# Message passing on a graph: fixed PSUM banks, overlapping stages and paired adding scatters in a kernel that sorts edges by target while it multiplies them

## The chip, the core and the metric

The kernel runs on one core of a Trainium2 chip. The metric is device time in microseconds (us), the median of three runs. The engines are TensorE (PE in the profile, its weight loads PEld), VectorE (DVE), ScalarE (ACT), GpSimd (POOL) and SyncE (SP, which only issues transfers here). POOL issues the indirect transfers: gathers and scatters whose rows are named by a list of indices.

## The reference: one layer of a message-passing network

```python
N, deg, D, De = 12500, 64, 64, 16
E = N * deg                                   # 800,000 edges
def reference(x, e_attr, src, dst, w_msg, w_upd):
    m_in = jnp.concatenate([x[src], x[dst], e_attr], axis=-1)
    msg = _silu(m_in @ w_msg)                 # (E, 64)
    agg = _segment_sum(msg, dst, N)           # (N, 64)
    return _silu(jnp.concatenate([x, agg], axis=-1) @ w_upd)
```

Everything is float32; `src` and `dst` are random, so an edge may go from any node to any node.

## The kernel before

The product with `w_msg` is split. `A = x @ w_msg[0:64]` is computed once per node and kept in DRAM (`A_d`); an edge gathers its source's row of it. The part of the target node and of the edge's attributes is a product of its own, with weights `BW` that hold 98 target nodes (a *bucket*; there are 128 buckets) and the 16 attribute rows. For this the edges have to lie sorted by bucket, and the kernel sorts them itself, with matrix products, while it works on those that are sorted already.

**Sorting.** 782 steps take 8 tiles of 128 edges each. A step makes a one-hot matrix of the buckets (`onehot`, ACT L396/L397), counts with bf16 matmuls which edge is the how-manieth of its bucket (`count`, PE, tile `z`), takes the rank by a maximum (`ranks`, DVE L433), spreads each edge's record of 17 floats to the slot of its rank (`expand`, DVE L446, tile `X`), and multiplies with the one-hot matrix (`move`, PE L463, tile `pl`), so that each of the 128 buckets has its records in one row of PSUM. The products of 8 tiles (the first 140 *chunks*) or of 12 (the other 428) are summed there. ACT copies the row block out (`blk`, L468), DVE moves each bucket's pointer on (`place`, L481/L482), and POOL scatters the 128 rows behind the buckets' ends in the store `st` in DRAM (L486): 24 or 30 records a row. A bucket that gets more records than a row holds loses the chunk, which is then redone at the end.

**Messages.** From the store, *groups* of 24 to 64 sorted tiles are taken. A group is formed over several periods (`k` = 0, 1, 2, ...): DVE computes how many whole units of 1, 2 or 4 tiles each bucket holds; a matmul with a triangular matrix (L581) makes running sums; three small matmuls make the *work list* (L585 to L587: the tile, the column of `BW` and the column of the sum for each unit), which DVE copies into `row` and `rb` (L592, L593); SP reads addresses from it and loads the tiles (`rt`). A group is worked on in *batches* of 8 tiles (6 in the second stage). A batch passes through four periods: 8 gathers by POOL (L649) and the one-hot matrix `q` of the targets within the bucket (DVE L659); transposes on PE (`tq`, L668), copied out by ACT (`qt`, L671), and the product `pre` with BW (PE L677); the sum with the gathered rows and SiLU (DVE L681, ACT L682); the reduction over targets by PE (`ag`, L698), added into `ACC` in SBUF (DVE L710).

**Order.** The program is issued exactly as it is written, engine by engine. One `period` holds a sort step and a batch, each in its present phase of the pipeline, in this order: four gathers, the scatter, four gathers; one-hot matrices; the small vector work of a group that is forming (`fourth`); counts; transposes and their copy; reduction; ranks; message; `add`; `expand`; `move`; `product`; the rest of `move`; `place`; the list matmuls of a forming group (`middle`). A planner written in Python decides before the program is built in which period a group starts, from 16 random draws of how full the buckets are. The early stages are 48 tiles one by one, then groups of 24 tiles two by two until each bucket has given its share, then groups of 64 tiles four by four; a stage starts when the one before has been taken whole. After the last sort step the left-over tiles run in a tail without sorting.

**PSUM.** Six pools of one buffer each hold `z`, the constants' bank `cb`, `pl`, `tq`, `pre` and `ag`. The work list's tile `ps` comes from the pool of `ag`:

```python
g.ps = pag.tile([P, 512], F32, name="ps2", tag="ag")     # the list of a forming group
t.ag = pag.tile([P, 512], F32, name="ag")                # the sums of a batch
```

so a list is written only when the sums before it have been added, and the next sums only when the list has been copied out. Four buffers of gathered rows are used in turn: the first gather into one waits for the last matmul of the `ag` that read it (`t.older`). Each matmul of `ag` is on record in `t.gathers`.

Of the kernel before, what the change touches and what calls it, by code (L numbers as in the profile page):

```python
# [14 lines left out]
P = 128  # L15
# [14 lines left out]
XR = 2 + W  # L30
# [6 lines left out]
FIRST = [(1, 48, BT, (1, 0, 1, 0)), (2, 24, 6, (3, 3, 2, 2))]  # L37
# [7 lines left out]
SUMMED = "the sum that this reads waits for the gathers into its buffer, the older ones there were read ahead of them"  # L45
LISTED = "the work list holds buckets and tiles of the store"


def mpnn_kernel(tc, x, e_attr, src, dst, w_msg, w_upd, out):
# [7 lines left out]
    CAPT = (K8 * S8 + (NCH - K8) * S) // P + 2  # L57
# [3 lines left out]
    NREC = TOP * P  # L61
# [11 lines left out]
    with es:  # L73
# [4 lines left out]
        pz = pool("pz", 1, space=PSUM)  # L78
        pc = pool("pc", 1, space=PSUM)
        pp = pool("pp", 1, space=PSUM)  # L80
        pt = pool("pt", 1, space=PSUM)
        ppre = pool("ppre", 1, space=PSUM)
        pag = pool("pag", 1, space=PSUM)

        A_d = dr.tile([NB * BK, D], F32, name="A_d")
        XU_d = dr.tile([BK, NBK * D], F32, name="XU_d")
        st = dr.tile([NREC, R], F32, name="st")
        st_t = st.rearrange("(t e) c -> t (e c)", e=P)

# [32 lines left out]
        cb = pc.tile([P, 512], F32, name="cb")  # L122
        ioB = cb[:, 0:BK]
        ioS = cb[:, BK:BK + S]
        hit = cb[:, P:P + M * S].rearrange("p (k s) -> p k s", s=S)
# [3 lines left out]
        nc.vector.tensor_scalar(out=ioS, in0=iof[:, 0:S], scalar1=RK, scalar2=None, op0=OP.add)  # L129

# [7 lines left out]
        ub = {u: cp.tile([NBK, 1], F32, name=f"ub{u}") for u in (1, 2, QU)}  # L138
        nc.vector.tensor_scalar(out=ub[1], in0=ipf, scalar1=float(CAPT), scalar2=None, op0=OP.mult)
        ptr0 = cp.tile([NBK, 1], I32, name="ptr0")  # L140
        nc.vector.tensor_scalar(out=ptr0, in0=ub[1], scalar1=float(P), scalar2=None, op0=OP.mult)
# [3 lines left out]
        capm = cp.tile([NBK, 2 + len(FIRST)], F32, name="capm")  # L145
# [8 lines left out]
        stages = []  # L154
        for i, (u, gt, bt, give) in enumerate(FIRST):
# [7 lines left out]
            stages.append(dict(u=u, gt=gt, bt=bt, cap=cap, caps=caps, total=u * sum(caps)))  # L163
        stages.append(dict(u=QU, gt=GT, bt=BT, cap=None, caps=None, total=None))
# [5 lines left out]
        class Nodes:  # L170
# [20 lines left out]
            def turn(t):  # L191

                xt_p = pt.tile([P, BT * P], F32, name="xt_p", tag="t")
# [9 lines left out]
            def parts(t, i):  # L203
                ps = (ppre, pag)[i % 2].tile([P, 512], F32, name="abp", tag=("pre", "ag")[i % 2])
# [132 lines left out]
        ACCf = ACC.rearrange("p b k -> p (b k)")  # L337
        for t in X:
            nc.gpsimd.memset(t[:, :, 0:1], 1.0)
        nc.gpsimd.memset(sent, 0.0)  # L340
# [6 lines left out]
        def later():  # L347
# [5 lines left out]
            if len(zeros) == 15:  # L353
                for k in range(P // SR):
# [7 lines left out]
        bp = pool("bp", 2)  # L362
        sm = pool("sm", 4)
        rcp = pool("rcp", 2)
# [6 lines left out]
        state = dict(x=0, rt=0, u=1, ptr=ptr0, done=done0, stage=0, taken=0, straight=True)  # L371

        blocks = []
        gathers = []
        live = []

        prior = dict(step=None, pl=None)

        class Step:


            def __init__(c, hi, rec, index, n=M):

                c.hi, c.rec, c.n = hi, rec, n
# [4 lines left out]

                c.last = {k: K8 + (index * M + k) // c.size for k in range(n) if c.pos[k] == c.size - 1}  # L390
# [27 lines left out]
            def count(c):  # L418

                hb = c.hf.bitcast(BF16).rearrange("p m (b two) -> p m b two", two=2)[:, :, :, 1]  # L420
                c.z = pz.tile([P, M, NBK], F32, name="z")
# [293 lines left out]
        def period(step=None, batch=None, ptr_new=None):  # L715
# [49 lines left out]
            if p:  # L765
                p.move(1)
# [420 lines left out]
```

## Time and profile before

| | |
|---|---|
| three runs | 10704.04, 10711.36, 10720.38 us; median 10711.36 |
| span of the profiled execution | 10886.0 us, at a mean granted TensorE clock of 0.885 |
| busy, share of the span | PE 82%, DVE 66%, POOL 60%, PEld 57%, ACT 47% |
| moved by DMA | 501.15 MB, 46 GB/s |
| gathers, scatters | 6322 and 568 |
| batches (copies `qt`), groups (pairs of list copies) | 818, 115 |

The profiled execution took 1.6% longer than the median of the three runs. In rows of groups, the number after x counts instructions; a float32 matmul is two records on PE, so 12644 records of `ag` are 6322 matmuls. Behind the bar stand the busy time in us and the mean of one in ns, then the time that the engine was idle just before, with what ended it. "remote" is a semaphore event that the profile doesn't put down to one instruction, "issue" is idle time in which the engine waited for nothing that the profile shows. Rows by stretch of time show the length, the busy time of each engine with its number of instructions, the granted clock, the share of the DMA engines' time and GB/s.

### The profile page before, as it was taken

How to read it: one execution, taken by the hardware profiler on the slowest of the kernel's cores; microseconds unless marked ns; L12 is line 12 of the kernel's file. 1: busy time of each engine (PE TensorE's matmuls, PEld its weight loads, DVE VectorE, ACT ScalarE, POOL GpSimd, SP SyncE). 2: the span in 40 equal slices, each digit the busy share in tenths (PEclk: the TensorE clock that was granted, in tenths of full speed). 3: DMA queues.
4: the chain of work that ended last, by engine and by line, in shares of the span. 5: the costliest groups of instructions: out<-in, count | busy, mean ns of one | idle time of the engine just before them, and what ended most of it. 6: DMA issues, size and time to landing. Idle time of an engine off the chain costs nothing. (4 is left out here: it accounts for less than half of the span.)

```text
span 10886.0 us, 155616 instructions
## 1 busy us (share of the span) xinstructions
PE 8949.9 (82%) x49053; PEld 6219.2 (57%) x49816; DVE 7231.4 (66%) x15936; ACT 5082.6 (47%) x12594; POOL 6571.4 (60%) x6908
## 2 busy tenths in 40 slices
PE   8788888888888888888888888888888888888556
PEld 5566655555555555555555555555555555555555
DVE  7777776666666666766666666666666666766232
ACT  6455554444444444444444444444444444544211
POOL 2565666666666666666666666666666666666555
PEclk9999998999989988999998999999899998988555
DMA  3111111111111111111111111111111111111212
GB/s 97 44 49 48 49 49 46 43 47 42 47 42 46 45 44 45 44 43 44 46 43 46 44 44 43 46 47 43 45 42 46 43 47 44 44 45 41 46 36 44
DMA packets 662903, 501.15 MB, mean 46 GB/s; under 512 B 492983, under 2 KB 529911, under 8 KB 662071
## 3 DMA queue, kind: packets, MB, share of 16 engines
q0 software_dynamic: 238976, 349.72, 12.3%
q1 hardware_dynamic: 422775, 141.27, 5.9%
q8 instruction: 400, 6.55, 0.3%
q14 instruction: 432, 3.54, 0.1%
q10 hardware_dynamic: 320, 0.07, 0.0%
HBM read 330.05 MB, written 152.30 MB: 44 GB/s over the span
## 5 line engine op out<-in xcount | busy, mean ns | idle before, releaser
L649 POOL DMA_INDIRECT g<-A_d,sidx x6322 | 5997.6, 949 | 3658.7 <-issue 1620.7
L463 PE MATMUL pl<-X,hf 128*128 128x291 f32 (+5 forms) x12512 | 4745.0, 524 | 476.4 <-issue 428.3
L463 PEld LDWEIGHTS pl<-X,hf 128*128 128x128 f32 x12512 | 2538.7, 211 | 2159.4 <-issue 1737.4
L446 DVE TENSOR_TENSOR X<-cb,rec 128x442 f32<-128x442 f32 (+5 forms) x3128 | 2646.6, 908 | 26.7
L396 ACT ACTIVATE hf<-iof,shi 128x128 f32<-128x128 f32 x6256 | 1908.8, 389 | 1360.4 <-PE pl L463 449.0
L671 ACT ACTIVATE qt<-tq 114x1024 f32<-114x1024 f32 (+1 forms) x818 | 811.7, 992 | 2951.3 <-remote 2298.5
L433 DVE TENSOR_REDUCE rank<-z 128x8 f32<-128x1024 f32 x782 | 954.5, 1221 | 1270.3 <-remote 874.9
L677 PEld LDWEIGHTS pre<-w,qt 114*128 114x128 f32 x10496 | 1392.5, 209 | 687.8 <-ACT qt L671 467.1
L677 PE MATMUL pre<-w,qt 114*128 114x64 f32 x10496 | 1395.2, 291 | 345.6 <-ACT qt L671 317.6
L710 DVE TENSOR_TENSOR ACC<-ag,ACC 64x98 f32 x1938 | 496.7, 256 | 1553.3 <-remote 1131.7
L698 PE MATMUL ag<-q,g 128*64 128x98 f32 x12644 | 882.3, 276 | 490.4 <-remote 236.2
L698 PEld LDWEIGHTS ag<-q,g 128*64 128x64 f32 x12644 | 681.6, 151 | 668.8 <-issue 381.7
L668 PE MATMUL tq<-ident,q 128*114 128x128 f32 x6322 | 929.9, 294 | 103.3 <-issue 91.5
L668 PEld LDWEIGHTS tq<-ident,q 128*114 128x114 f32 x6322 | 812.6, 147 | 238.7 <-issue 122.6
L397 ACT ACTIVATE hf<-hf,ones 128x1024 f32<-128x1024 f32 x782 | 898.8, 1149 | 25.4
L486 POOL DMA_INDIRECT st<-blk,ptrs x567 | 567.2, 1000 | 561.4 <-ACT blk L468 272.2
L659 DVE TENSOR_TENSOR q<-cb,lo 128x784 f32<-128x784 f32 (+1 forms) x818 | 768.7, 940 | 96.1 <-PE ag L698 46.3
L468 ACT ACTIVATE blk<-pl 128x512 f32<-128x512 f32 (+1 forms) x568 | 324.9, 572 | 818.2 <-PE pl L463 500.9
L426 PE MATMUL z<-G,onesb 128*128 128x384 bf16 x1564 | 529.8, 339 | 78.9 <-issue 25.2
L682 ACT ACTIVATE g<-g 128x512 f32<-128x512 f32 (+1 forms) x818 | 498.4, 609 | 192.5 <-DVE g L681 111.8
L681 DVE TENSOR_TENSOR g<-pre,g 128x512 f32<-128x512 f32 (+1 forms) x818 | 541.3, 662 | 51.4 <-issue 37.2
L677 PE MATMUL pre<-BW,qt 114*128 (+1 forms) x2148 | 326.3, 314 | 99.0 <-ACT qt L671 64.8
(138 smaller groups left out, 5243.9 us busy)
## 6 DMA issues: line engine op xcount, KB each, us to landing
g<-A_d,sidx POOLq DMA_INDIRECT x6322
ea<-in_e_attr SPq DMA_DIRECT2D x260, 192.0 KB
rt<-st SPq DMA_DIRECT2D x1312, 34.0 KB
st<-blk,ptrs POOLq DMA_INDIRECT x567
rt<-st SPq DMA_DIRECT2D x434, 8.5 KB
nodes<-in_x SPq DMA_DIRECT2D x62, 98.0 KB
ACC<-rt SPq DMA_DIRECT2D x11, 544.0 KB
rt<-st SPq DMA_DIRECT2D x320, 17.0 KB
```

Of the source, the lines that this page charges most:

```text
L396: nc.scalar.activation(c.hf[:, k, :], iof, AF.Square, bias=c.hi[:, k:k + 1])
L397: nc.scalar.activation(c.hf, c.hf, AF.Relu, bias=ones, scale=-1.0)
L433: nc.vector.tensor_reduce(out=c.rank, in_=c.z, axis=AX.X, op=OP.max)
L446: nc.vector.tensor_tensor(out=c.x[:, k:k + 2, 2:2 + n * R].rearrange("p k (s c) -> p k s c", c=R), in0=hit[:, k:k + 2, 0:n, None].to_broad ...
L463: nc.tensor.matmul(pl[:, 0:w], c.hf[:, k, :], c.x[:, k, 0:w], start=(n == (c.size - 1 if whole else 0)), stop=ends, skip_group_check=True)
L486: i = nc.gpsimd.indirect_dma_start(out=st, out_offset=bass.IndirectOffsetOnAxis(ap=c.ptr, axis=0), in_=c.blk[:, 2:], in_offset=None)
L649: j = nc.gpsimd.indirect_dma_start(out=t.g[:, i, :], out_offset=None, in_=A_d, in_offset=bass.IndirectOffsetOnAxis(ap=t.grp.sidx[:, k:k + ...
L659: nc.vector.tensor_tensor(out=t.q[:, 0:n, 0:BK], in0=ioB[:, None, :].to_broadcast([P, n, BK]), in1=t.grp.lo[:, i0:i0 + n, None].to_broadca ...
L668: nc.tensor.transpose(t.tq[0:KQ, j * P:(j + 1) * P], t.q[:, j, :], ident)
L671: nc.scalar.activation(t.qt[:, 0:w], t.tq[0:KQ, 0:w], AF.Copy)
L677: nc.tensor.matmul(t.pre[:, i * D:(i + 1) * D], t.qt[:, i * P:(i + 1) * P], w, start=True, stop=True)
L698: o = nc.tensor.matmul(t.ag[t.half(v), v // 2 * BK:(v // 2 + 1) * BK], t.g[:, i, :], t.q[:, i, 0:BK], start=(k == 0), stop=(k == u - 1))
```

## The change

There are three parts.

1. **PSUM tiles are held for good.** `z`, `tq`, `pl`, `pre`, `ag` and `cb` are allocated once. The work list gets columns 400 to 512 of the `ag` bank to itself when it has at most 112 entries; a longer one still takes the whole bank (64 units at one tile each have 192). With it, the matmuls of `ag` are no longer on record one by one: one more matmul per batch, eight columns by one, stands behind them and is what gathers and additions wait for.
2. **Stages overlap.** The single tiles come first and are 192, in groups of 12, 12 and 24 tiles with batches of 6. Each stage keeps its own account of what it has taken, and in each period the first stage that has enough for a group starts one. The groups of four-tile units are 32, 32, 32 and then 64 tiles.
3. **Chunks past step 140 go to the store in pairs.** The first of two chunks is laid flush right in a row of 30 records, the second flush left in the 30 beside it, and one scatter writes rows of 60 records so that both lie end to end behind the bucket's end. What lies around them are zeros, and the scatter adds to what is in DRAM instead of overwriting it. The rows have to hold zeros beforehand: SP copies a block of zeros (`Z_d`, 128 rows of 4080 bytes) to each part of the store, four parts ahead. A pair in which a bucket lost records is scattered aside.

```diff
+XR = 2 + W + 2
+ROW = 2 * S
+LEAD = 4
-FIRST = [(1, 48, BT, (1, 0, 1, 0)), (2, 24, 6, (3, 3, 2, 2))]
+FIRST = [(1, (12, 12, 24), 6, (2, 1, 2, 1)), (2, (24,), 6, (3, 3, 2, 2))]
+LATER = (32, 32, 32, GT)
...
-        pag = pool("pag", 1, space=PSUM)
+        ps = pool("ps", 1, space=PSUM)
+        zb = ps.tile([P, M, NBK], F32, name="z")
+        tb = ps.tile([P, BT * P], F32, name="tq")
+        plb = ps.tile([P, 512], F32, name="pl")
+        preb = ps.tile([P, 512], F32, name="pre")
+        agb = ps.tile([P, 512], F32, name="ag")
...
+        def fill():
+            a = (P - S + len(filled) * ROW) * R
+            z = nc.sync.dma_start(st_b[:, a:a + ROW * R], Z_d)
...
+            def keep(c, pl, right):
+                if c.single or c.side == 0:
+                    prior["cnt"] = sm.tile([NBK, 8], F32, name="cnt")
...
+                if c.main:
+                    nc.scalar.activation(c.cnt[:, c.side, :], pl[:, f:f + 2], AF.Copy)
+                c.blk = BLK[:, c.side, 0:n]
+                nc.scalar.activation(c.blk, pl[:, a:a + n], AF.Copy)
...
             def scatter(c):
-                i = nc.gpsimd.indirect_dma_start(out=st, out_offset=bass.IndirectOffsetOnAxis(ap=c.ptr, axis=0), in_=c.blk[:, 2:], in_offset=None)
+                if c.single:
+                    i = nc.gpsimd.indirect_dma_start(out=st, out_offset=at, in_=c.blk, in_offset=None)
+                else:
+                    i = nc.gpsimd.indirect_dma_start(out=st, out_offset=at, in_=BLK.rearrange("p a w -> p (a w)"), in_offset=None, compute_op=OP.add)
...
+        def listing(n):
+            return agb[:, 4 * BK + 8:512] if n <= 504 - 4 * BK else agb
...
-                    g.ps = pag.tile([P, 512], F32, name="ps2", tag="ag")
+                    g.ps = listing(3 * gu)
...
             def reduce(t):
-                t.ag = pag.tile([P, 512], F32, name="ag")
+                t.ag = agb
...
-                            o = nc.tensor.matmul(t.ag[t.half(v), v // 2 * BK:(v // 2 + 1) * BK], t.g[:, i, :], t.q[:, i, 0:BK], start=(k == 0), stop=(k == u - 1))
-                            t.gathers.append(o.ins)
+                            nc.tensor.matmul(t.ag[t.half(v), v // 2 * BK:(v // 2 + 1) * BK], t.g[:, i, :], t.q[:, i, 0:BK], start=(k == 0), stop=(k == u - 1))
+
+                o = nc.tensor.matmul(t.ag[0:t.n, 4 * BK:4 * BK + 1], t.g[:, 0:t.n, 0], ones, start=True, stop=True)
+                t.gathers.append(o.ins)
...
-            if size() and may_start() and draws.holds(state["u"], size() // state["u"]):
...
+            if may_start():
+                for g in stages:
+                    n = size(g)
+                    if n and draws.holds(g, n):
+                        draws.take(g, n)
+                        start_group(g, state["ptr"], n)
+                        break
```

How the instructions stand, at three places. First, PE behind the list of a forming group (L585 to L587 write the list of 16 units, `z` counts, `tq` transposes, `ag` is the reduction). Before:

```order
L585 MATMUL ps_33559<-mat,wl 1x16 [waits DVE_49]
L586 MATMUL ps_33559<-mat,b_102 1x16
L587 MATMUL ps_33559<-mat,b_104 1x16
L428 LDWEIGHTS onesb
L428 MATMUL z<-G,onesb 128x512 [waits DVE_49]
L668 MATMUL tq<-ident,q 114x128 x8
L698 MATMUL ag<-q,g_223 64x98 [waits DMASW6_49,DVE_49,PE_49]
L698 MATMUL ag<-q,g_223 64x98 [waits DMASW3_49]
```

The same place now, where the list is L677 to L679, the reduction L790 and the added matmul L792:

```order
L677 MATMUL ag<-mat,wl 1x16 [waits DVE_49]
L678 MATMUL ag<-mat,b_93 1x16
L679 MATMUL ag<-mat,b_95 1x16
L475 LDWEIGHTS onesb
L475 MATMUL z<-G,onesb 128x512 [waits DVE_49]
L760 MATMUL tq<-ident,q 114x128 x8
L790 MATMUL ag<-q,g_233 64x98 [waits DMASW1_49,DVE_49]
L790 MATMUL ag<-q,g_233 64x98 [waits DMASW0_49]
L792 MATMUL ag<-ones,g_233 8x1
L516 MATMUL pl<-X_193,hf 128x359 x2
```

The wait of `ag` for PE's own list matmuls is gone, and what its wait for DVE now stands for is no longer the copies of the list, only the messages and the additions of the batch before. The matmul L792 is new in every batch.

Second, POOL in the stretch with both kinds of work (`st` is the store, `g` gathered rows). Before, and in most periods:

```order
L486 DMA st<-blk,ptrs 2938112x17 [waits DMASW3_49,DMASW4_49,DVE_49,Activation_49]
L649 DMA g_220<-A_d,sidx 128x64
L649 DMA g_220<-A_d,sidx 128x64 [waits DMASW5_49]
L649 DMA g_221<-A_d,sidx 128x64 [waits DMASW6_49,PE_49]
L649 DMA g_221<-A_d,sidx 128x64 [waits DMASW7_49]
L649 DMA g_221<-A_d,sidx 128x64 [waits DMASW0_49]
```

Now, with an adding scatter in every third period, which also waits for a fill of zeros (DMAHW):

```order
L570 DMA st<-BLK,cnt 2994944x17 [waits DMASW1_49,DMAHW0_49,DVE_49,Activation_49]
L741 DMA g_234<-A_d,sidx 128x64 [waits DMASW2_49]
L741 DMA g_234<-A_d,sidx 128x64 [waits DMASW3_49]
L741 DMA g_234<-A_d,sidx 128x64 [waits DMASW4_49]
L741 DMA g_234<-A_d,sidx 128x64 [waits DMASW5_49]
L741 DMA g_235<-A_d,sidx 128x64 [waits DMASW6_49,PE_49]
```

The semaphores DMASW0 to DMASW7 are taken in turn, so that each gather waits until the indirect transfer eight places before it has landed; 354 scatters are left of 568.

Third, SP, which loads the groups' tiles (`rt`) and now also writes the zeros:

```order
L661 DMA rt_198<-st 128x34 [waits DMAHW3_49]
L276 DMA sdi<-in_dst 128x72 [waits DMAHW4_49]
L276 DMA ssi<-in_src 128x72 [waits DMAHW5_49,DVE_49]
L415 DMA st<-Z_d 128x1020 [waits DMAHW3_49,DMAHW6_49,DMAHW2_49,DMAHW7_49,DMAHW1_49,DMAHW0_49]
L276 DMA ea<-in_e_attr 128x384 [waits Activation_49]
L577 TENSOR_LOAD row [waits DVE_49]
L661 DMA rt_199<-st 128x34 [waits DMAHW6_49,DMASW6_49]
```

The row `st<-Z_d` is new, 271 times; it waits for the loads of tiles before it, and the next load waits for it.

In counts, the sort steps without a batch go from 28 to 24. The batches beside a sort step go from 754 (8 of eight single tiles, 107 of the two-tile stage, 639 of eight in fours) to 758 (32 of six single tiles, 107, 619); the tail goes from 64 batches to 68, and the groups from 115 to 122.

More of the change, by code (lines that the diff above doesn't have):

```diff
@@ L29 @@
 W = S * R
-XR = 2 + W
+XR = 2 + W + 2
+ROW = 2 * S
+LEAD = 4
 BT = 8
@@ L45 @@
 SUMMED = "the sum that this reads waits for the gathers into its buffer, the older ones there were read ahead of them"
+AHEAD = "the zeros are written ahead of the rows that any bucket can have reached; a scatter waits for those that it may reach"
 LISTED = "the work list holds buckets and tiles of the store"
@@ L388, in __init__ @@
                 c.prev, prior["step"] = prior["step"], c
+                c.right = [not main or c.turn == 2 or c.turn == 3 or (c.turn == 1 and k >= C - M) for k in range(M)]
                 c.last = {k: K8 + (index * M + k) // c.size for k in range(n) if c.pos[k] == c.size - 1}
```

317 lines of the change are left out of this document (193 added, 124 removed).

## The prediction

> **What bounds the kernel now.** I read the busy shares first, then the stretches of the steady part, then what each engine waited for. The page begins with the span and the shares:
>
> ```profile
> span 10886.0 us, 155616 instructions
> PE 8949.9 (82%) x49053; PEld 6219.2 (57%) x49816; DVE 7231.4 (66%) x15936; ACT 5082.6 (47%) x12594; POOL 6571.4 (60%) x6908
> ```
>
> 82% is a mean; the stretches say more. The first two rows are everything in a piece of the steady part and in the tail; the other four count the ranks (L433, one a sort step) and then, for the tail, the copies `qt` (L671, one a batch):
>
> ```profile
> 3000.00:5000.00 2000.00, 1680.19 (x9200) 1139.71 (x9350) 1366.67 (x2886) 961.18 (x2400) 1238.64 (x1301) 0.91 0.17 44
> 10100.00:10700.00 600.00, 355.54 (x2070) 307.55 (x2072) 159.49 (x455) 110.52 (x227) 354.30 (x376) 0.55 0.21 39
> ...
> 0.00:200.00 200.00, 29.36 (x24) 0.97 0.45 116
> 600.00:1400.00 800.00, 87.64 (x72) 0.92 0.20 49
> 3000.00:5000.00 2000.00, 183.11 (x150) 0.91 0.17 44
> 10100.00:10700.00 600.00, 47.83 (x48) 0.55 0.21 39
> ```
>
> So a period costs 200/24 = 8.3 us without a batch, 800/72 = 11.1 us with six tiles, 2000/150 = 13.3 us with eight, and 600/48 = 12.5 us in the tail. Of the 13.3 us PE is busy 1680.19/150 = 11.2, DVE 9.1, ACT 6.4. PE is nearest to being the bound, with some 2 us a period in which it stands. What POOL needs is in three rows:
>
> ```profile
> L649 POOL DMA_INDIRECT g<-A_d,sidx x6322 | 5997.6, 949 | 3658.7 <-issue 1620.7
> L486 POOL DMA_INDIRECT st<-blk,ptrs x567 | 567.2, 1000 | 561.4 <-ACT blk L468 272.2
> POOL g L649 <- issue: 1620.7, 5211, 8.0
> ```
>
> A gather costs 0.95 + 1620.7/5211 = 0.31, so 1.26 us; eight of them and 568/782 of a scatter at 1.3 us are 11.0 us. POOL has 2.3 us of slack in a period. Now what PE and its neighbours wait for:
>
> ```profile
> ACT qt L671 <- remote: 2298.5, 540, 16.1
> DVE rank L433 <- remote: 874.9, 271, 16.3
> PE pl L463 <- issue: 428.3, 704, 5.9
> PE pre L677 <- ACT qt L671: 382.5, 134, 13.9
> PEld ag L698 <- remote: 251.2, 70, 5.7
> PE ag L698 <- remote: 236.2, 70, 5.5
> DVE row L592 <- remote: 175.2, 68, 5.0
> ...
> L698 PEldq EVENT_SEMAPHORE  x81: 2001/4893/7850, 1039.2 to 8906.4; - x81
> ```
>
> The last row, from the view of L698 between 1000 and 9000 us (minimum, median and maximum in ns), says that PE's sequencer stood ahead of `ag` 81 times. How that looks, from the timelines of PE and of DVE around one list:
>
> ```profile
> 2089.56 0.20 PE L587 MATMUL ps<-mat,b 128*1 128x16 f32 x2
> 2090.92 1.03 PE L668 MATMUL tq<-ident,q 128*114 128x128 f32 x8
> 2095.92 1.36 PE L698 MATMUL ag<-q,g 128*64 128x98 f32 x16 [3.97 <-remote]
> ...
> 2095.55 0.17 DVE L592 SCALAR_TENSOR_TENSOR row<-ps,iof 1x16 int32<-1x16 f32 x1 [2.70 <-remote]
> 2095.65 0.17 DVE L593 CAST rb<-ps 1x32 int32<-1x32 f32 x1
> 2097.05 1.23 DVE L433 TENSOR_REDUCE rank<-z 128x8 f32<-128x1024 f32 x1 [1.23 <-PE ag L698]
> ```
>
> PE wrote the list at 2089.6 and was through with `tq` at 2092; `ag` stood until DVE had copied the list at 2095.8, because list and sums share a bank. The ranks stood behind it too.
>
> **The change, part by part.** The sum is made against the profiled 10,886 us and then multiplied by 10,711/10,886 = 0.984 for the median.
>
> *The list's own columns* take this wait away: `ag` can follow `tq` at once. The direct price is the row of PE's idle time, **-236 us**. Bounds: 115 groups times the sequencer's 4.9 us is -563. At the other end another wait takes the place: what is late next is `qt`, whose wait costs PE 382.5/134 = 2.9 us each time it occurs; if each of the 70 stops of 3.4 us only moves there, 0.5 us of each is left, -35 us. I take the row, since in the timeline the ranks, which `expand` and the next `move` hang on, start once `ag` is released. Groups of 64 single tiles still wait, but they lie in the tail.
>
> *The added matmul* runs 826 times. It has eight columns of weights and one column to stream. The rows nearest to it are the list's own matmuls (one column of weights) and the running sum (128 columns, one streamed):
>
> ```profile
> 2089.46 0.20 PE L585 MATMUL ps<-mat,wl 128*1 128x16 f32 x2
> 2089.51 0.20 PE L586 MATMUL ps<-mat,b 128*1 128x16 f32 x2
> ...
> L581 PEld LDWEIGHTS cb<-wl,tri x230: 186/189/338, 158.2 to 10377.6; 128*128 128x128 f32 x115
> L581 PE MATMUL cb<-wl,tri x230: 223/271/374, 158.2 to 10377.7; 128*128 128x1 f32 x115
> ```
>
> From start to start the first take 0.05 us, +41 us in all; weights and matmul of the second, end to end, 0.46 us, +380 us. Eight columns are far nearer to one than to 128: I take 0.10 us, **+83 us**. PE is on the path, so nothing hides it. In exchange seven of eight completion events a batch are gone. I count nothing for this, but it is a rival below. The Trainium skill, TensorE: Matmul & The Clock Gate, section "The cost: per-tile semaphore tail", states 26.3 ns for each increment, and recommends one on the last matmul, as the change has it; an estimate from that page is 7 x 26.3 = 184 ns a batch, and a sum with it would be 152 us lower and 10,430 us at the median. No row of this trace shows the length of such a tail.
>
> *The schedule.* With the prices of the stretches: four sort steps fewer without a batch, -33; 32 batches of six single tiles for 8 of eight, 32 x 11.1 - 8 x 13.3 = +249; twenty fewer in fours, -266; four more in the tail, +50. Together **0**, with 40 us to either side for the prices. Seven more groups form. PE stands ahead of the running sum of each:
>
> ```profile
> L581 PE MATMUL cb<-wl,tri 128*128 128x1 f32 x230 | 50.7, 290 | 234.0 <-DVE X L446 70.1 <-issue 68.0 <-DVE wl L548 38.8
> ```
>
> 234/115 = 2.0 us, so **+14 us**.
>
> *The pairs.* POOL loses 214 scatters of 1.3 us, 278 us. It gains 0.4 us a period of a slack that it has already, so this is counted at **0** (were POOL the bound it would be all 278). ACT copies two counts more per chunk, 568 small copies; DVE has six small operations a pair for four. Their nearest rows:
>
> ```profile
> L468 ACT ACTIVATE blk<-pl x568: 492/589/601, 31.3 to 10051.8; 128x512 f32<-128x512 f32 x143, 128x410 f32<-128x410 f32 x47
> L482 DVE SCALAR_TENSOR_TENSOR ptrs<-blk,LOST,ptrs x567: 218/219/247, 42.6 to 10052.7; 128x1 int32<-128x1 f32 x189
> ```
>
> At 0.2 us, and at most 0.6, for a copy and 0.22 for two further operations ACT gains 114 to 340 us and DVE 47, beside 7 and 4 us of other idleness in each period. What hides them is PE's own work; without that cover they would be +160. Counted at 0.
>
> *Transfers.* SP writes 271 blocks of 522 KB, 141 MB, and reads as many; scatters move the same bytes in fewer, larger pieces, and an addition reads its target besides. What a byte costs:
>
> ```profile
> q0 software_dynamic: 238976, 349.72, 12.3%
> SPq L491 <- DVE rb L593: 3068.8, 53, 106.6
> SPq L491 <- DVE row L592: 1584.0, 20, 101.3
> ```
>
> 12.3% of 16 engines' 10,886 us over 349.72 MB are 61 engine-us per MB: a row block of 522 KB takes 2.0 us on 16 engines, 4.0 if the addition reads it first. The zeros add some 141 x 2 x 61 = 17,300 engine-us, 10% of the engines' time on top of 18%. SP's queue stood 4,650 us waiting for work lists in these two rows alone; a fill between two groups' loads fits there. The DVE copies come sooner now, so SP's loads do. Counted at 0. The self-waits of `z` and `tq` on their own earlier tiles go too; those tiles were a period old, 0.
>
> Sum: -236 + 83 + 0 + 14 = **-139 us**, 10,747 us profiled, times 0.984: **10,575 us**, 1.3% faster.
>
> **The rivals.** *B, the events were the wait.* PE stands 428.3 us, 704 times 0.6 us, ahead of `pl`, which follows `ag`, with nothing to wait for; and ranks and `qt` wait for "remote" events that come after `ag` was issued (1.23 us behind L698 in the timeline). If handing out eight completions does that, one event ends it: 10,886 - 139 - 428 = 10,319, 10,154 us at the median; with a third of it, 10,430. The Trainium skill's rule comes out at the same place. Against it: PE's weight loads stand 1,737 us for "issue" ahead of the same line, mostly where no `ag` is near:
>
> ```profile
> PEld pl L463 <- issue: 1737.4, 5457, 6.8
> ```
>
> *C, the wait moves to `qt`.* The low bound above: -35 + 83 + 14 = +62 us, 10,948 profiled, 10,773 us, slower by 0.6%. For it: ACT waits 2,298 us for `tq`, 4.3 us each time, and that is not touched. It decides if the first `pre` of the period after a list starts no sooner than now.
>
> *D, the added matmul is dear.* A weight load of another shape between `ag` and `pl` may cost as much as the running sum's: 0.46 us, +380 - 236 + 14 = +158, 11,044 profiled, 10,867 us. The matmul outweighs the list's gain from 0.27 us on.
>
> *E, the additions are slow.* A gather waits for the transfer eight places before it, 8 x 1.26 = 10.1 us, and POOL has 2.3 us of slack: nothing is lost until an adding scatter takes over 12.4 us to land. At 14 us, 214 x 1.6 = +342 us, 10,910 us at the median. It would have to take over three times the 4.0 us.
>
> **How the numbers follow.** The forecast has 0.55 (its own range 10,470 to 10,670: the bounds of the schedule, the groups and the matmul at 0.05 to 0.2 us), B 0.15, C 0.15, D 0.09, E 0.06. The range reaches into B to the third of its price and past C into D: 10,330 to 10,840 us leaves out half of B, E and most of D, 0.2 together. A measurement of this kernel tells 0.2% from no change, that is 10,690 to 10,733 us. Faster are B and nearly all of the forecast (0.66), slower C, D and E with a little less than their 0.30, since C comes near to no change (0.25); 0.09 is left for the same.
>
> **What would show it.** In the profile after: the waits of the reduction's line for "remote" are down from 236 us to a few, and no sequencer row of 4.9 us stands there but in the tail; the list copies on DVE come at their own place without holding PE. The added matmul stands at 0.05 to 0.2 us behind each reduction. POOL is busy some 210 us less (214 x 1.0) with the period no shorter for it. A period of the steady part, by ranks per 2000 us, is 13.1 instead of 13.3. B is right if the "issue" idleness ahead of `pl` shrinks to under half; C, if the wait of `pre` for `qt` grows by some 200 us; D, if the idleness between the reduction and `pl` grows by 0.3 us a batch; E, if POOL waits for DMA more than the present
>
> ```profile
> POOL g L649 <- DMA g<-A_d,sidx: 96.0, 315, 0.3
> ```
>
> The prediction is wrong in its reasons if the time falls while those waits of the reduction stay.

## The result: 1.6% slower, and where it was looked at again 0.3% faster

The changed kernel takes 10,880.81 us (median of four runs, 10,849.47 to 10,917.16), the kernel before beside it 10,713.81 (four runs). The ratio is 1.0158, with a 95% interval from 1.0135 to 1.0181. The forecast was 10,575 and the range ended at 10,840.

In four of the five later comparisons the same kernel before took 8,909 to 8,911 us, and in the fourth of them 10,723, so the work was done under two conditions, which are kept apart here by the time of the kernel before. In the first comparison and in the later one at 10,723 us, what waits for PE is released some microseconds late, which is called *late events* below; in the others it is released at once. Each later comparison ran on another chip (numbers 15, 12, 5 and 8 at 8,909 to 8,911 us, number 9 at 10,723; for the first comparison no number is on record). So the condition may belong to the chip or to what was going on around it: no run here tells these apart.

The page of the changed kernel in the first comparison, its busy shares, the two large DMA queues and the scatters of pairs:

```profile
span 10885.0 us, 162247 instructions
PE 9077.6 (83%) x51528; PEld 6289.9 (58%) x51528; DVE 7328.3 (67%) x17005; ACT 5100.4 (47%) x13146; POOL 6521.8 (60%) x6696
q0 software_dynamic: 242400, 349.71, 18.0%
q1 hardware_dynamic: 479367, 283.87, 9.9%
L570 POOL DMA_INDIRECT st<-BLK,cnt x214 | 348.2, 1627 | 627.5 <-ACT hf L443 245.8
```

POOL lost 50 us of busy time, not the 214 that 214 scatters at 1.0 us should have freed: an adding scatter keeps POOL for 1.63 us, and the gathers took 30 us more. SP's queue carries 143 MB more, as expected.

The wait that the forecast was built on, from the view of the reduction's line (L790); the numbers behind the event instruction are minimum, median and maximum in ns, those below are idle us and how often, for PE and its weight loads together:

```profile
L790 PEldq EVENT_SEMAPHORE  x183: 51/51/13397, 226.1 to 10869.7; - x183
  issue: 1146.0, 1710
  DVE rb L685: 209.9, 126
```

**The wait for the list's copies is still there.** "DVE rb" is the copy of the work list. The part of the change's description that says it is no longer waited for was a misreading of the order: the row there shows "DVE" among the waits of the reduction, and the list's copy is still one of the things waited for; only the wait for PE's own list matmuls is gone. In PE's own rows 236.2 us (put down to "remote", 70 times) became 96.0 (60 times). The time did not fall with it. Four rows of waiting, two that rose and two that fell:

```profile
PE ag L790 <- issue: 476.8, 522, 11.2
DVE rank L480 <- remote: 986.2, 194, 10.0
PE pl L516 <- issue: 231.8, 330, 2.8
PE pre L769 <- ACT qt L763: 245.2, 98, 11.4
```

Before, these were 229.7 us (207 times), 874.9, 428.3 and 382.5.

**These two profiles can't show where the 167 us went.** The profile of the kernel before lasted 10,886.0 us, 1.6% more than its timed runs; that of the change lasted 10,885.0 and is one of its timed runs. Their rows compare two executions of the same length. The last rank stands at 10,036.8 us before and at 9,998.0 in the change, and what follows it takes 849 and 887 us.

What late events do to a step is seen in a timeline. This is one step of the changed kernel in which one chunk ends and the next begins, PE first (with the reduction of the batch before for comparison) and then DVE:

```profile
4993.72 0.90 PE L790 MATMUL ag<-q,g 128*64 128x98 f32 x16
...
5003.01 0.81 PE L790 MATMUL ag<-q,g 128*64 128x98 f32 x13
5004.94 0.24 PE L790 MATMUL ag<-q,g 128*64 128x98 f32 x1 [1.13 <-issue]
5005.68 0.24 PE L790 MATMUL ag<-q,g 128*64 128x98 f32 x1 [0.49 <-issue]
5007.09 0.32 PE L790 MATMUL ag<-q,g 128*64 128x98 f32 x1 [1.17 <-issue]
5007.79 0.16 PE L792 MATMUL ag<-ones,g 128*8 128x1 f32 x1 [0.38 <-issue]
5009.18 0.16 PE L792 MATMUL ag<-ones,g 128*8 128x1 f32 x1 [1.23 <-issue]
5009.90 1.69 PE L516 MATMUL pl<-X,hf 128*128 128x461 f32 x2 [0.56 <-issue]
...
5012.08 1.22 DVE L480 TENSOR_REDUCE rank<-z 128x8 f32<-128x1024 f32 x1 [9.12 <-remote]
```

From 5005 us on PE starts one record, half a float32 matmul, every 0.7 to 1.4 us, where 16 of them took 0.90 us in the batch before; it waits for nothing that the profile shows. DVE waits 9 us for counts that PE had issued by 5002. The distance between two ranks there is 18.6 us. By the place in a cycle of three steps the mean distances of the changed kernel are 10.5 to 10.8, 15.6 to 16.0 and 13.1 to 13.2 us; of the kernel before, in its profile, 12.9 to 13.1, 13.8 and 13.1 to 13.2 (worked out from all ranks from the 145th on). In these two profiles the change shortens one step in three by 2.3 us and lengthens another by 2.0.

### The profile page after: what moved, and what is told of

It is laid out like the page before. It is cut to its first block, busy times and chain, and to the rows that moved or that the text cites. A ratio compares the mean times of both kernels' runs of the same rounds, so it can differ in the third digit from the quotient of the medians.

```text
span 10885.0 us, 162247 instructions
## 1 busy us (share of the span) xinstructions
PE 9077.6 (83%) x51528; PEld 6289.9 (58%) x51528; DVE 7328.3 (67%) x17005; ACT 5100.4 (47%) x13146; POOL 6521.8 (60%) x6696
## 5 line engine op out<-in xcount | busy, mean ns | idle before, releaser
L516 PE MATMUL pl<-X,hf 128*128 128x291 f32 (+5 forms) x12512 | 4615.6, 518 | 278.8 <-issue 231.8
L516 PEld LDWEIGHTS pl<-X,hf 128*128 128x128 f32 x12512 | 2492.4, 206 | 1794.2 <-issue 1332.5
L769 PEld LDWEIGHTS pre<-w,qt 114*128 114x128 f32 x10176 | 1326.2, 204 | 559.2 <-issue 297.5
L769 PE MATMUL pre<-w,qt 114*128 114x64 f32 x10176 | 1319.2, 285 | 241.8 <-ACT qt L763 170.9
L790 PE MATMUL ag<-q,g 128*64 128x98 f32 x12644 | 964.4, 276 | 591.4 <-issue 476.8
L790 PEld LDWEIGHTS ag<-q,g 128*64 128x64 f32 x12644 | 711.3, 150 | 816.0 <-issue 669.3
L570 POOL DMA_INDIRECT st<-BLK,cnt x214 | 348.2, 1627 | 627.5 <-ACT hf L443 245.8
L540 ACT ACTIVATE cnt<-pl 128x2 f32<-128x2 f32 x568 | 96.8, 170 | 1191.5 <-PE pl L516 578.4
L472 PE MATMUL z<-hf,w 128*128 128x512 bf16 x1564 | 638.4, 408 | 1.0 <-issue 1.0
```

Source lines behind the costliest of these rows:

```text
L472: nc.tensor.matmul(c.z[:, k:k + ZB, :], w1, hb[:, k:k + ZB, :], start=True, stop=False)
L516: nc.tensor.matmul(pl[:, a - o:b - o], c.hf[:, k, :], c.x[:, k, a:b], start=(n == (c.size - 1 if whole else 0)), stop=ends, skip_group_che ...
L769: nc.tensor.matmul(t.pre[:, i * D:(i + 1) * D], t.qt[:, i * P:(i + 1) * P], w, start=True, stop=True)
L790: nc.tensor.matmul(t.ag[t.half(v), v // 2 * BK:(v // 2 + 1) * BK], t.g[:, i, :], t.q[:, i, 0:BK], start=(k == 0), stop=(k == u - 1))
```

## The experiments

Each ratio is to the kernel before, run beside it.

| kernel | us | beside it | ratio (95%) |
|---|---|---|---|
| the change, first comparison | 10,880.8 | 10,713.8 | 1.0158 (1.0135 to 1.0181) |
| the kernel before again | 8,911.6 | 8,909.4 | one run |
| the change again | 8,881.2 | 8,910.1 | 0.9966 (0.9952 to 0.9979) |
| fixed tiles alone | 8,918.4 | 8,910.1 | 1.0011 (1.0002 to 1.0020) |
| fixed tiles, added matmul | 8,924.3 | 8,911.0 | 1.0016 (1.0006 to 1.0025) |
| fixed tiles, new stages | 8,937.7 | 8,911.0 | 1.0030 (1.0019 to 1.0042) |
| fixed tiles, pairs | 8,850.7 | 8,910.1 | 0.9933 (0.9918 to 0.9948) |
| the change without pairs | 8,951.4 and 8,948.0 | 8,909.4 and 8,910.7 | 1.0047 (1.0030 to 1.0064), 1.0042 (1.0028 to 1.0056) |
| the change without the added matmul | 8,870.8 | 8,909.4 | 0.9959 (0.9945 to 0.9973) |
| the change with the stages of before | 8,849.0 | 8,909.4 | 0.9931 (0.9915 to 0.9948) |
| the change, four added matmuls | 8,896.9 | 8,911.0 | 0.9983 (0.9973 to 0.9992) |
| the change, scatter first | 8,857.4 | 8,910.1 | 0.9942 (0.9926 to 0.9957) |
| fixed tiles, pairs, scatter first | 8,811.7 | 8,911.0 | 0.9890 (0.9873 to 0.9906) |
| the change, pairs not added | 9,219.4 | 8,910.7 | 1.0346 (1.0331 to 1.0360) |
| the kernel before, PE loaded | 11,071.0 | 10,722.6 | 1.0318 (1.0300 to 1.0337) |
| the change, PE loaded | 11,513.7 | 10,722.6 | 1.0730 (1.0712 to 1.0748) |
| ... without the added matmul | 11,460.6 | 10,722.6 | 1.0681 (1.0663 to 1.0699) |
| ... without the pairs | 11,077.6 | 10,722.6 | 1.0328 (1.0306 to 1.0349) |

### The kernel before, once more

No edit.

> The kernel before, profiled once more, since the profile that the prediction was read from took 10,886 us where the timed runs took 10,704 to 10,720. If that profile was a disturbed execution, the new one has a span near 10,715 us, a granted clock above 0.885, and waits of the reduction for its list well under 236 us; if profiling itself costs 1.6% here, the span is 10,886 us again.

Its page and three of its rows of waiting:

```profile
span 8909.8 us, 156379 instructions
PE 8221.1 (92%) x49816; PEld 5875.1 (66%) x49816; DVE 7248.8 (81%) x15936; ACT 5060.9 (57%) x12594; POOL 6585.1 (74%) x6908
ACT qt L671 <- PE tq L668: 345.9, 129, 7.5
POOL g L649 <- DMA g<-A_d,sidx: 250.2, 821, 0.3
DVE g L681 <- DMA g<-A_d,sidx: 751.6, 462, 19.3
```

Neither expectation had thought of 8,910 us. DVE, ACT and POOL are busy for as long as in the first profile (7,249, 5,061 and 6,585 us beside 7,231, 5,083 and 6,571), so their instructions take the same time; what has gone is waiting. PE is the exception: it is busy 729 us less than in the first profile and idle 1,247 us less. ACT waits 346 us for `tq` where it waited 2,298 for something "remote". The rows of the reduction in this profile hold

```profile
L698 PE MATMUL ag<-q,g 128*64 128x98 f32 x12644 | 773.0, 263 | 45.8 <-issue 24.1
```

45.8 us of idleness in place of 490.4. The prices that the forecast took from the first profile, 236 us for the list and 428 us ahead of `pl`, are prices of late events. How late they are can be read from what waits for them (medians over the waits, worked out from the two traces). In the first profile the rank starts 4.2 us behind the end of the last counts (511 waits), and `qt` 5.0 us behind the end of the last `tq` (710 waits). In this profile both start 0.04 us behind (122 and 130 waits). ACT's copy of `pl` starts 0.04 us behind PE and ACT's SiLU 0.03 us behind DVE's sum in both profiles, so not every event is late. The ends of matmuls are modelled, so these figures can't tell an event that is late from a matmul that ended late.

The traces themselves differ too. This one holds 99% of the landing events of POOL's transfers, the first profile 25%. Every trace of the first condition, the change's and those of the loaded kernels below included, holds 25 to 35%, and every other one about 99%. So "remote" in the first profile is in part an event that the trace lacks. Whether the recording of events has a part in the delay is not shown.

### One part undone at a time

Three kernels; the edits are

```diff
# without pairs
-c.right = [not main or c.turn == 2 or c.turn == 3 or (c.turn == 1 and k >= C - M) for k in range(M)]
+c.right = [True] * M
-c.single = index < K8
+c.single = True
# and no fills
```

```diff
# without the added matmul
-nc.tensor.matmul(t.ag[...], t.g[:, i, :], t.q[:, i, 0:BK], ...)
-o = nc.tensor.matmul(t.ag[0:t.n, 4 * BK:4 * BK + 1], t.g[:, 0:t.n, 0], ones, start=True, stop=True)
-t.gathers.append(o.ins)
+o = nc.tensor.matmul(t.ag[...], t.g[:, i, :], t.q[:, i, 0:BK], ...)
+t.gathers.append(o.ins)                     # for each
```

```diff
# the stages of before
+FIRST = [(1, (48,), BT, (1, 0, 1, 0)), (2, (24,), 6, (3, 3, 2, 2))]
+LATER = (GT,)                               # and a stage only after the one before
```

> The changed kernel with chunks past step 140 scattered one by one as before: no pairs, no zeros, no additions; fixed PSUM tiles, the added matmul and the overlapping stages stay. Theory P (the pairs cost the time: zeros and additions load the DMA engines, 28% in place of 18%, and more small operations on ACT and DVE): back to 10,715 us, perhaps 10,700. Theory M (the added matmul costs it, 0.2 us a batch on a path that PE sets): 10,880 us, or 10,900 with the 214 scatters back on POOL. Theory S (the schedule costs it): 10,880 us.

> The changed kernel without the added matmul: each matmul of the reduction is on record again, as before, and gathers and additions wait for those. P: 10,870 us. M: 826 x 0.2 us fewer, 10,715 us. S: 10,870 us. If eight events cost more than the matmul, it gets slower: 10,950 us.

> The changed kernel with the stages of before: 48 single tiles in one group with batches of eight, a stage only after the one before, groups of 64 from the start. P and M: 10,880 us, within 30. S: 10,715 us. By the prices of the stretches the schedules cost the same, within 40 us.

All three ran beside 8,909 us, where the change was not yet known. With the next runs (8,881 for the change) they read: the pairs **gain** 70 us, the added matmul costs 10 (the ratios' intervals overlap), the new stages cost 32. None is a loss of 167 us.

### The change again, and two parts alone

The change without edit; then only fixed tiles with the list's columns; then those with the pairs.

> The changed kernel itself, timed again, since in the first comparisons the kernel before took 8,909 us and a clean profile (granted clock 0.94, PE 92% busy, no late events), not 10,714 (0.885, 82%). Theory H (how the change stands depends on how late PE's events come): beside a kernel before of 8,909 us the change is no slower, 8,880 to 8,910; beside 10,714 it is slower again by 1.5%. Theory N (the change is slower by itself): 1.3 to 1.8% slower than the kernel before in either case.

> Only the first part of the change without the added matmul: PSUM tiles held for good and the list in its own columns; no pairs, the stages of before, each matmul of the reduction on record. If the list's columns took the wait away, this is 1.5 to 2% faster than before; if the wait for the list's copies is still in the program, it equals before within 0.3%. The reduction's wait for the list copies (line L790) tells directly.

> The pairs with fixed tiles; the stages of before and no added matmul. By the first runs (taking out the added matmul and taking the old stages back each gave an 8,849 to 8,871 us kernel where leaving out the pairs gave 8,951) this is the fastest: 8,810 to 8,840 beside 8,909, near 1% faster. Theory P (pairs cost time) has it slower than before by 1%.

Beside 8,910 us the change is 0.34% faster, as theory H has it. H's other half, that without load it is slower again beside 10,714, met no later comparison that could test it. Fixed tiles alone change nothing that counts (+8 us). That time can't decide about the list's columns, since with prompt events PE hardly waits there; but the reduction still waits for the list's copies:

```profile
L789 PEldq EVENT_SEMAPHORE  x173: 51/51/2227, 312.6 to 8904.9; - x173
  DVE rb L684: 78.4, 94
```

The pairs alone are 68 us faster than fixed tiles alone, less than expected. Where this comes from is in the waits of the two, fixed tiles first:

```profile
DVE g L772 <- DMA g<-A_d,sidx: 664.5, 440, 7.6
...
DVE g L773 <- DMA g<-A_d,sidx: 216.6, 52, 8.1
```

With PE's events prompt, POOL is near to being the bound and messages wait for gathered rows. An estimate from the rows: eight gathers at 1.26 us and two thirds of a scatter at 1.3 are 10.95 us a step without pairs, eight gathers and one third of an adding scatter at 1.63 + 0.3 are 10.72 with them. Between 3,000 and 8,000 us a step takes 10.89 us with fixed tiles alone and 10.73 with the pairs. At 13.3 us a step the same relief was counted at nothing.

### Two more parts alone, and the sum

The added matmul on fixed tiles, and the new stages on fixed tiles; edits as above, the other way round.

> Fixed tiles and the added matmul; no pairs, the stages of before. Where the kernel before takes 8,910 us, the differences of the earlier runs give 8,918 for the fixed tiles plus -2 to +10 for the matmul: 8,916 to 8,928. Where it takes 10,714 us and PE's events come late, theory M (there PE's own time is the bound) gives +140 to +170 us over before, 10,850 to 10,885; if the matmul is harmless there too, 10,714 to 10,740.

> Fixed tiles and the overlapping stages; no pairs, no added matmul. Beside 8,910 us: 8,918 plus the 20 to 32 us that the stages cost in the other pairs of runs, 8,938 to 8,950. Four more batches in the tail (11 us each there) are most of it. Beside 10,714: four tail batches at 12.5 to 13.5 us, +50, 10,765; theory S has all of the change's loss here, 10,880.

8,924 and 8,938: +6 and +19 over the fixed tiles. Beside 8,910 us the parts add up roughly: fixed tiles +8, matmul -2 to +10, stages +19 to +32, pairs -67 to -70 make -45 to -17, and -29 was measured. Which stretch each part changes is seen by the times of the ranks in the four profiles, in us:

| kernel | first rank to the 145th | from there to the last | behind the last rank |
|---|---|---|---|
| fixed tiles alone | 1,282 | 6,925 | 695 |
| fixed tiles, new stages | 1,322 | 6,913 | 694 |
| fixed tiles, pairs | 1,302 | 6,806 | 721 |
| the change again | 1,349 | 6,788 | 728 |

The stages cost 40 us in the first steps, where the single tiles run. **The longer tail is not theirs, as the second expectation above has it, but the pairs':** 70 batches stand behind the last rank with pairs and 65 or 66 without, whichever the stages. The planner counts a pair's records only when its second chunk is placed, which would make the last groups start later. Against these 26 us stand some 119 that the pairs gain in the steps past the 145th.

### Four added matmuls

```diff
-o = nc.tensor.matmul(t.ag[0:t.n, 4 * BK:4 * BK + 1], t.g[:, 0:t.n, 0], ones, start=True, stop=True)
+for _ in range(4):
+    o = nc.tensor.matmul(t.ag[0:t.n, 4 * BK:4 * BK + 1], t.g[:, 0:t.n, 0], ones, start=True, stop=True)
```

> The changed kernel with the added matmul issued four times in place of once: 2,478 more of them. The profile gives one 0.09 us of weights and 0.16 of matmul. If PE sets the pace, each costs 0.1 to 0.2 us: 250 to 500 us more than the change, 9,130 to 9,380 beside 8,910. If PE has slack where it stands, under 50 us more.

+16 us for 2,478 matmuls, 0.006 us each. A PE that is busy 92% of the span has slack for them where they stand: here the busiest engine is not the bound.

### The scatter first

```diff
-if q: q.gather(0, BT // 2)
-if s: s.scatter()
-if q: q.gather(BT // 2, BT)
+if s: s.scatter()
+if q: q.gather(0, BT)
```

> The changed kernel with the scatter ahead of the first four gathers of a period instead of behind them. In the profiles with pairs ACT's copy into the block waits for the pair's scatter to have been read (453 to 469 us) and PE's next sum for the copy (279 to 308 us). A scatter five us sooner ends most of that: if this wait sets the period, 100 to 250 us faster than the change itself; if POOL then stands for the block's copy instead, or the wait was covered, no faster.

24 us faster than the change, not 100 to 250. A wait that the prediction had missed stands behind it: there is one block `BLK` of two sides where there were two buffers, so ACT's next copy waits until the pair's scatter has read it. The change, and then with the scatter first:

```profile
ACT BLK L542 <- DMA st<-BLK,cnt: 445.3, 197, 3.7
PE pl L516 <- ACT BLK L542: 272.9, 181, 2.9
...
ACT BLK L542 <- DMA st<-BLK,cnt: 301.1, 174, 3.3
PE pl L516 <- ACT BLK L542: 167.4, 132, 2.4
```

105 us of PE's waiting went, and a quarter of it came back as time. A second block, which would take the wait away whole, was not tried.

> The pairs without the other two parts' costs (stages of before, no added matmul) and with the scatter ahead of the gathers: the two gains found so far together, 8,851 - 24 = 8,827 us beside 8,910, 0.9% faster than before; if they are one and the same gain, 8,850. Beside 10,714: faster than before by 0.5 to 1% if the pairs are good there too, slower by 1% if they are what costs there.

This combination (fixed tiles, pairs, stages of before, no added matmul, scatter first) took 8,812 us, 1.1% faster than the kernel before. The gain of the scatter first is 39 us here. It was not run where events come late.

### PE loaded in both kernels

```diff
+for _ in range(5):
+    nc.tensor.matmul(c.z[:, k:k + ZB, :], w1, hb[:, k:k + ZB, :], start=True, stop=True)
 nc.tensor.matmul(c.z[:, k:k + ZB, :], w1, hb[:, k:k + ZB, :], start=True, stop=False)
```

> The kernel before with ten more counting matmuls (128x512, bf16) in each of the 782 steps, each written over by the next, so that PE is the bound with near 2.2 us more a step (0.22 us each by their spacing). If PE sets the pace, 782 x 2.2 = +1,720 us, 10,600; the slack that PE has now comes off, so 10,200 to 10,600.

> The changed kernel with the same ten matmuls a step. Theory B (the change loses wherever PE is the bound, because the added matmul then costs its 0.1 to 0.2 us 826 times and the POOL time that the pairs save is worth nothing): 0.8 to 1.6% slower than the loaded kernel before. Theory L (the first comparison's loss comes from PE's late events and low clock, not from PE being the bound): within 0.4% of the loaded kernel before, or faster.

> The loaded changed kernel without the added matmul. B: faster than the loaded change by 80 to 160 us. L: within 20 us of it.

> The loaded changed kernel without the pairs. Where POOL was the partner in setting the pace, leaving out the pairs cost 70 us; under the load it costs nothing by B (within 20 us of the loaded change, and faster if the pairs cost PE waits), and 70 us by L.

These four met the condition of the first comparison: 10,723 us beside them, and late events (in the loaded kernel before, the rank starts 1.9 us behind the counts, the median of 733 waits). **The loaded change is 443 us slower than the loaded kernel before (4.0%, 11,514 over 11,071), and without the pairs that loss is gone: 11,078.** The added matmul is worth 53 us. Both theories fail: PE's time is not the bound (7,820 matmuls added to the kernel before cost 348 us, while PE was busy with them for 2,050), and most of the loss is not in the added matmul but in the part that POOL was relieved by. The steps per 5,000 us, between 3,000 and 8,000 us, by the ranks: the loaded kernel before, the loaded change, the loaded change without pairs,

```profile
3000.00:8000.00 5000.00, 453.98 (x371) 0.98 0.19 44
...
3000.00:8000.00 5000.00, 436.24 (x357) 0.95 0.26 55
...
3000.00:8000.00 5000.00, 454.95 (x372) 0.99 0.19 44
```

13.48, 14.01 and 13.44 us a step. The pairs bring more DMA (26% in place of 19%) and a lower clock (0.95 in place of 0.99). By the place in the cycle of three, the change's steps take 12.5 to 12.9, 16.3 to 16.6 and 12.9 to 13.0 us, without pairs 12.0, 14.7 and 13.5 to 13.6, and those of the loaded kernel before 12.2 to 12.3, 14.4 to 14.5 and 13.7. The same step swells by some 2 us as in the first comparison's profiles; what differs is that here the step before it gets no shorter. Of the 436 us that the pairs cost, 37 are in the longer tail.

### The pairs without load, and without the addition

No new edit for the first; for the second

```diff
-in_=BLK.rearrange("p a w -> p (a w)"), in_offset=None, compute_op=OP.add)
+in_=BLK.rearrange("p a w -> p (a w)"), in_offset=None)
```

> The changed kernel without the pairs, without load, once more. Beside a kernel before of 8,910 us it took 8,951 (0.5% slower); there this says nothing new. Beside 10,714 to 10,723, theory P2 (where PE's events come late, the pairs are the whole loss) gives 10,700 to 10,740, within 0.3% of before, 140 to 180 us faster than the change's 10,881; if the pairs matter there only under the extra load, it stays at 10,860 or more.

> The changed kernel with its pairs scattered plainly in place of added; the zeros are written as before. (The addition is left out, so a row's zeros write over records of the pair before.) Everything else stands where it stood. Beside a kernel before of 8,910 us: if the addition itself costs anything there, faster than the change's 8,881 by up to the 200 us of PE's waits for the block; else the same. Beside 10,714 to 10,723: if the addition (6 us to land, it reads and writes the store) is what holds PE up in every third step, 10,720 to 10,760; if it is the 141 MB of zeros or the pairs' order of work, 10,860 to 10,900.

Both met 8,911 us beside them, so the question that they were for stays open. The first repeats 8,951 (8,948). The second is 338 us slower than the change, which nobody had expected, and is no measure of the addition: without it many records of the store are zeros, which name row 0 of `A_d`, and POOL's transfers, gathers for the most part, took the DMA engines' time. The queue of POOL's transfers in the change and here:

```profile
q0 software_dynamic: 242400, 349.71, 21.4%
...
q0 software_dynamic: 228704, 349.71, 56.4%
```

That the repeated row is the reason is argued, not shown.

## Why the prediction was wrong

**The list's own columns, -236 us.** This step failed twice. The change does not remove the wait: list and sums still share a bank, and the reduction still waits for the list's copies. I had seen the wait for PE's own matmuls vanish from the order's rows and read the "DVE" that remained as the messages, without following its value to the instruction that it waits for. That the change might not do what it says was not among the rivals. The Trainium skill states the rule that should have stopped me, in PSUM — Partial Sum Buffer, section "PSUM bank collisions raise a hardware error": PSUM is to be guarded by bank and quadrant, not by address, since disjoint columns of one bank collide too. The list lies in the bank and in partitions of the sums, so by that rule the wait has to stay; the rows of L790 agree (209.9 us behind "DVE rb"), and no run here took the wait away. Second, the 236 us were a price of the condition in which PE's events come late; with prompt events PE stands there 45.8 us in all, for every reason. The timeline in the prediction shows it already: PE had written the list by 2089.8 us, and DVE's copy, for which the reduction stood, began at 2095.55 behind a "remote" wait of its own.

**The added matmul, +83 us.** Beside 8,910 us it costs -2 to +10; with late events and under load 53, in both cases less what one event in place of eight saves, which no run separates. The size is about right for the latter, within the bounds of 41 and 380. The cost fell outside the bounds where PE has slack, since the argument "PE is on the path, so nothing hides it" does not hold there. Rival D is refuted beside 8,910 us, where a further one costs 0.006 us; with late events only the balance of 53 us is known. Rival B gained nothing on balance in either condition (8,871 without the added matmul, 8,881 with it; 11,461 and 11,514). The idleness ahead of `pl` did fall, from 428.3 us to 231.8, not quite to the half that B asked for, and 247 us came up ahead of `ag` instead. The estimate of 152 us that the prediction worked out from the Trainium skill (TensorE: Matmul & The Clock Gate, "The cost: per-tile semaphore tail", 26.3 ns for each increment) is not to be seen in this balance. Beside 8,910 us PE's idle time ahead of `pl` is 4.8 us in the whole kernel before, so there was no tail on the path to save.

**The schedule, 0, and seven groups, +14.** Measured +19 to +32, within the bounds, but not for the reason given: the stages cost their 40 us in the first steps, and the tail's four batches come from the pairs.

**The pairs, 0.** This is the term that decides. With prompt events the pairs gain 67 to 70 us, because there POOL and its gathers are in the path. With late events and the load they cost 436 us. The prediction had looked for a loss at POOL (rival E: the transfer eight places before); POOL waits for DMA less than before in the first comparison (68.9 us in place of 96.0), and an adding scatter lands 6.1 us (median) after its start, not 12.4 or more. So E's mechanism is not it, though the part of the change that E blamed is. The prediction had also overlooked the wait for the one block; putting the scatter first took part of it away and gave back 24 to 39 us. Rival C's sign is absent too: the wait of `pre` for `qt` fell, from 382.5 us to 245.2.

**The first comparison's 167 us.** This is only argued, and the cause stays open: the pairs are the sole part shown to cost that much with late events, and that was under load. The run that would have shown it, the change without pairs and without load, met the other condition. The first profiles can't stand in for it: that of the kernel before is as long as the change's, so its step of 13.3 us need not be that of the timed runs. The predicted step of 13.1 us was even met (13.16, by 380 ranks in 5,000 us), but by coincidence, since the wait that was to shorten it stayed. And why PE issues slowly in the step after a pair is not settled: scatter, fill of zeros and the large loads repeat every three steps together, and alignment in time can't tell them apart.

## What to carry to other kernels

A profile's wait is a price only in the condition in which it was taken. Before a term is built on "remote" waits and on idle time that waits for nothing, see that the profile is as long as the timed runs, see how many of the expected events its trace holds, and profile the kernel a second time. When a change is to remove a wait, follow the semaphore's value to the instruction that it counts; the engine's name in the row isn't enough, and columns of their own within one PSUM bank took no wait away here. A part that relieves one engine with extra transfers can be a gain or a loss by which engine is waited for that day, so time the parts one by one, and see by stretch where each part's time goes.

## What the runs showed of the hardware

- The same program took 8,910 us or 10,714 to 10,723, with DVE, ACT and POOL busy equally long. The difference is in when what waits for PE is released (medians of 4.2 and 5.0 us behind the counts and `tq`, or 0.04), in PE's busy time (8,950 us, or 8,221), in PE's clock (0.885, or 0.941), and in how much the trace holds (25% of the landing events of POOL's transfers, or 99%).
- The clock alone does not make the condition: in the loaded kernel before it was 0.98 between 3,000 and 8,000 us, and a step took 13.48 us with the rank 1.9 us late; in the unloaded one with prompt events it was 0.96, and a step took 10.9.
- With late events, 7,820 extra matmuls of 128x512 in bf16, 2,050 us of PE's busy time, cost 348 us, and PE's mean clock rose from 0.885 to 0.949.
- An adding scatter of 128 rows of 4,080 bytes holds POOL for 1.63 us, the same scatter without addition for 1.00:

```profile
L570 POOL DMA_INDIRECT st<-BLK,cnt x214: 1622/1629/1737, 1367.1 to 8188.5; - x107
...
L570 POOL DMA_INDIRECT st<-BLK,cnt x214: 997/999/1209, 1363.9 to 8444.2; - x107
```
